# Attention and two feed-forward blocks on one core: one transpose for both heads' first 64 keys

## The chip, the cores and the metric

The kernel runs on one core of a Trainium2 chip. The metric is device time in microseconds (us). The kernel before takes 504.18 us, the median of 3 runs (503.7 to 505.47).

## The reference

Causal attention over 2 sequences of 448 tokens with 12 heads of 64, then two feed-forward blocks on the 896 tokens of width 768. All inputs and outputs are fp32.

```python
# attention: q, k, v are (2, 12, 448, 64)
scores = np.matmul(q, k.transpose(0, 1, 3, 2)) / np.sqrt(64)
scores = np.where(np.triu(np.ones((448, 448), bool), k=1), -1e9, scores)
scores = scores - scores.max(-1, keepdims=True)
attn = np.exp(scores)
attn = attn / (attn.sum(-1, keepdims=True) + 1e-09)
x = np.matmul(attn, v).transpose(0, 2, 1, 3).reshape(896, 768)
# first block: w_in (768, 2048), w_out (2048, 768), alpha (2048,)
h = x @ w_in
y = (np.maximum(h, 0) + alpha * np.minimum(h, 0)) @ w_out
# second block: w1, w2, w3, w_out2 (768, 768)
out = np.maximum(np.maximum(y @ w1, y @ w2), y @ w3) @ w_out2
```

## The kernel before, in words

Nothing is issued in the order in which it is written. Each step (a load, a group of matmuls, one elementwise instruction) is given to a planner (`Plan`, L71) with a rank, the engines that could run it and a cost on each, the steps it follows, and the ring buffers it takes and gives back. `Plan.run` (L146) then issues, again and again, the step that can start first on its clock, and among equals the one with the lowest rank. The order on each engine is fixed when the kernel is built; at run time an engine takes its own list in order and waits on semaphores.

Attention is 12 jobs (`Job`, L463), one for a sequence and a pair of heads j = 0, 1. The 448 queries are cut into four chunks c of 64, 128, 128 and 128 rows (`START`, L228), and the keys in the same way. Because the mask is causal, chunk c has scores with its first `START[c+1]` keys alone: 64, 192, 320 or 448. A job goes through these steps:

- Two loads: `qk` (448 KB, L558) and `v` (256 KB, L562), from SyncE's queue.
- Scores (`scores`, L564) in two steps of two chunks, first 448 and 64 columns, then 320 and 192. The two heads use the two halves of TensorE's rows, 64 each, side by side. A step takes two of four PSUM banks (ring `s`).
- For each chunk and head: the masked row maximum on VectorE (L595), the exponential with its row sum on ScalarE (L608), per step one reciprocal on VectorE (L619, L620), and the scaling on GpSimd (L624). All of this is in place in the tile `e`, which holds first all of head 0, then all of head 1.
- Transposes (`p_t`, L633) by TensorE, in three groups per head: the first 64 keys (4 transposes that give 64 rows), key chunks 1 and 3 (4), and key chunk 2 (2). That is 20 per job. Each group is copied from PSUM (ring `t`, 3 banks) to the tile `p` by VectorE (L287) or ScalarE (L281): 6 copies per job. The upper half of the rows of the first group in `p` is zeroed once (L449).
- The product with V (`av`, L648, called AV below): 8 matmuls, for the 4 key chunks and the 2 heads, of 448, 384, 256 and 128 columns. The two heads use the two halves of TensorE's columns, side by side. The result is split in two parts for the next block (`xh` L281, `xl` L293).

Every fp32 matmul of scores and AV stands in the trace as two records (two passes); a transpose is one.

The feed-forward blocks multiply split numbers: each product is three matmuls (L406), high by high, high by low and low by high. A weight matrix is split by ScalarE and VectorE (and sometimes GpSimd) into such a pair, in a ring of four (`w`). Products of w_in whose weights are ready early are put between the steps of the last jobs (fill). After attention TensorE does the rest of the first block, the second block and the stores; the 896 tokens go as a piece of 512 and one of 384 columns, always in this order.

At the start TensorE does 8 products on a tile of zeros (`warm`, L711), which VectorE has to write first (L259). A small load brings `alpha` on ScalarE's queue (L274).

Of the kernel before, what the change touches and what calls it, by code (L numbers as in the profile page):

```python
# [23 lines left out]
RINGS = dict(w=4, m=1, s=4, t=3, v=4, qk=3, e=3, p=4)  # L24
NB = 5
HELD = 4
WARM = 8
# [3 lines left out]
    load=-6, s=12, max=12, exp=16, recip=10,  # L31
# [39 lines left out]
class Plan:  # L71
# [27 lines left out]
    def add(  # L99
        self, rank, engines, fn, after=(), take=(), give=(), delay=0.0, port=False, mode="full"  # L100
    ):
# [6 lines left out]
        self.waiting[i] = (rank, engines, fn, after, tuple(take), give, delay, port, mode)  # L108
        self.open[i] = sum(d in self.waiting for d in after)
        for d in after:  # L110
            self.next.setdefault(d, []).append(i)
        if not self.open[i]:
            self.ready[i] = None
        return i

    def start(self, step):
# [12 lines left out]
        for engine, took in engines.items():  # L129
# [6 lines left out]
            if engine == "PE" and mode != self.mode:  # L136
# [9 lines left out]
    def run(self):  # L146
        while self.waiting:
# [20 lines left out]
            if engine == "PE":  # L168
                self.mode = mode
# [18 lines left out]
def attention_moe_moe2_kernel(  # L188
# [73 lines left out]
    mask = first.tile([P, S], F32, name="mask")  # L262
    nc.gpsimd.memset(mask, 0.0)
    nc.gpsimd.affine_select(
        out=mask[:, S - P :],
        in_=mask[:, S - P :],
        compare_op=ALU.is_ge,
        fill=FILL,
        base=0,
        pattern=[[-1, P]],  # L270
        channel_multiplier=1,
    )
    alpha_sb = const.tile([P, KF], F32, name="alpha_sb")
    nc.scalar.dma_start(out=alpha_sb, in_=alpha)  # L274
# [133 lines left out]
    class Product:  # L408


        def __init__(self, rank, pieces, bank, token):

            total = len(pieces)
            self.end = None
            for i, (count, n, terms, after, give) in enumerate(pieces):
                self.end = plan.add(
                    rank,
# [19 lines left out]
    BANKS = ((0,), (1, 3), (2,))  # L437
    AT_COL, BANK_COL = {}, [0]
# [7 lines left out]

    p_all = [at.tile([P, BANK_COL[-1]], F32, bufs=1, name=f"p{i}") for i in range(RINGS["p"])]
    for p in p_all:
        nc.vector.memset(p[ROWS[0] :, : BANK_COL[1]], 0.0)  # L449
# [4 lines left out]
    e_all = [at.tile([P, 2, NP], F32, bufs=1, name=f"e{i}") for i in range(RINGS["e"])]  # L454
    for e in e_all:
        nc.vector.memset(e[ROWS[0] :, :, : OFF[1]], 0.0)
    used = {"p": 0, "e": 0}
# [5 lines left out]
    class Job:  # L463


        def __init__(self, rank, b, hp):
            self.b, self.hp = b, hp
            self.ps, self.pt, self.p = {}, {}, {}

            def add(kind, *args, **kw):  # L470
# [3 lines left out]
            load_v = add("load", on_dma(256), step(self.load_v), take=("v",), delay=1.8)  # L474

            norm = [[], []]
            s = None
            for i, cs in enumerate(PAIRS):
# [7 lines left out]
                    give=(("qk", load_qk),) * (i == len(PAIRS) - 1),  # L486
# [21 lines left out]
                for c in cs:  # L508
                    for j in range(2):
                        took = on_pool(START[c + 1], two=False)  # L510
                        if b * HP + hp < FIRST:
                            took |= on_dve(START[c + 1], fast=True)
                        norm[j].append(
                            add("norm", took, partial(self.normalize, i, c, j), (r,), port=True)
# [3 lines left out]
            for j in range(2):  # L518
                for n in range(len(BANKS)):
                    w = BANK_COL[n + 1] - BANK_COL[n]  # L520
                    keys = sum(ROWS[kc] for kc in BANKS[n] for c in range(kc, NCH))
                    t = add(
                        "p",
                        {"PE": keys * 0.85e-3 + 0.03},
                        step(self.p_t, j, n),
                        norm[j] if t is None else [*norm[j], t],
                        take=("t",) + ("p",) * (n == 0),
                        give=(("e", e_took),) * (j == 1 and n == len(BANKS) - 1),
                    )
                    if n == 0:  # L530
                        p_took.append(t)
                    src = partial(self.pt.get, (j, n))
                    outs.append(
                        add(
                            "p_out",
                            on_dve(w, psum=True) | on_act(w, psum=True),
                            copy(partial(self.p_part, j, n), src),
                            (t,),
                            give=(("t", t),),
                        )  # L540
                    )
            a = add(
                "av",
                {"PE": 4 * BANK_COL[-1] / 2400},
# [3 lines left out]
                mode="columns",  # L548
                give=(*(("p", x) for x in p_took), ("v", load_v)),
# [14 lines left out]
        def scores(self, i):  # L564
# [6 lines left out]
            for c in PAIRS[i]:  # L571
                n = START[c + 1]
                for j in range(2):
# [7 lines left out]
                        self.qk[d, 1, :n],  # L581
# [5 lines left out]
        def e_part(self, c, j):  # L587
            return self.e[: ROWS[c], j, OFF[c] : OFF[c + 1]]

        def column(self, tile, i, c, j):  # L590
            return tile[: ROWS[c], 2 * i + PAIRS[i].index(c), j : j + 1]

        def row_max(self, i, c, j):
            n, m = START[c + 1], S - P + ROWS[c]
# [3 lines left out]
                in1=mask[: ROWS[c], m - n : m],  # L598
# [18 lines left out]
        def recip(self, i):  # L617
            sm = self.sm[:, 2 * i : 2 * i + 2, :]
# [14 lines left out]
        def p_t(self, j, n):  # L633
            if n == 0:
                self.p[j] = turn("p", p_all)
            keys = ROWS[BANKS[n][0]]
            pt = ps_t.tile([P, BANK], F32, tag="t", name="pt")
            self.pt[j, n] = pt[:keys, : BANK_COL[n + 1] - BANK_COL[n]]
# [374 lines left out]
```

## Time and profile before

| | |
|---|---|
| median of 3 runs | 504.18 us |
| the profiled execution | 504.13 us, span 502.3 us (1.8 us lie around the span) |
| attention, first scores to last AV | 4.25 to 101.03 us |
| feed-forward matmuls after it | 101.03 to 498.97 us |
| TensorE busy | 495.1 us, 99% of the span |
| ScalarE, VectorE, GpSimd busy | 256.9, 360.6, 63.5 us |

The busy time of TensorE is modelled, so the chain of waits is read beside it: it tells which engine the end of the program depended on at each time. PE is TensorE's matmul, PEld its loading of the stationary operand, DVE is VectorE, ACT is ScalarE, POOL is GpSimd, SP is SyncE. In the tables x16 means 16 records merged.

### The profile page before, as it was taken

How to read it: one execution, taken by the hardware profiler on the slowest of the kernel's cores; microseconds unless marked ns; L12 is line 12 of the kernel's file. 1: busy time of each engine (PE TensorE's matmuls, PEld its weight loads, DVE VectorE, ACT ScalarE, POOL GpSimd, SP SyncE). 2: the span in 40 equal slices, each digit the busy share in tenths (PEclk: the TensorE clock that was granted, in tenths of full speed). 3: DMA queues.
4: the chain of work that ended last, by engine and by line, in shares of the span. 5: the costliest groups of instructions: out<-in, count | busy, mean ns of one | idle time of the engine just before them, and what ended most of it. 6: DMA issues, size and time to landing. Idle time of an engine off the chain costs nothing.

```text
span 502.3 us, 7218 instructions
## 1 busy us (share of the span) xinstructions
PE 495.1 (99%) x2684; PEld 427.5 (85%) x2684; DVE 360.6 (72%) x727; ACT 256.9 (51%) x502; POOL 63.5 (13%) x113
## 2 busy tenths in 40 slices
PE   8999999999999999999999999999999999999997
PEld 5665666789989899898899899898899899889997
DVE  7889878859999999968557467579999896601000
ACT  5999898645453555434425335366566544401111
POOL 3657755330100000000000000000000000000000
PEclk9999999999999999999999999999999999999999
DMA  7635410213332333333333343253554443000111
GB/s 255 234 88 173 154 44 13 111 67 125 127 126 78 112 127 105 116 115 106 115 116 104 93 138 122 69 185 128 188 186 160 157 134 118 1 1 31 64 64 63
DMA packets 14147, 56.70 MB, mean 113 GB/s; under 512 B 1696, under 2 KB 3488, under 8 KB 14112
## 3 DMA queue, kind: packets, MB, share of 16 engines
q1 hardware_dynamic: 13968, 56.24, 33.7%
q8 instruction: 21, 0.34, 0.3%
q14 instruction: 14, 0.11, 0.1%
q10 hardware_dynamic: 144, 0.01, 0.0%
HBM read 53.49 MB, written 2.75 MB: 112 GB/s over the span
## 4 chain that ended last, share of the span: by engine, by line
PE 94%; DVE 3%; ACT 2%; issue 0%; DVEq 0%
PE ps L406 81%; PE pt L643 4%; PE pv L652 4%; PE ps L578 4%; DVE e L595 2%; ACT e L608 1%; DVE sm L619 1%; PE warm L714 1%; DVE p L287 0%; ACT p L281 0%; DVE sm L620 0%; ACT o L281 0%; DVE nm L595 0%; ACT xh L281 0%; DVE zeros L259 0%
## 5 line engine op out<-in xcount | busy, mean ns | idle before, releaser
L406 PE MATMUL ps<-xh,wh 128*128 128x384 f32 (+2 forms) x408 | 149.4, 366 | 0.0
L406 PE MATMUL ps<-xh,wl 128*128 128x384 f32 (+2 forms) x408 | 148.7, 364 | 0.0
L406 PE MATMUL ps<-xl,wh 128*128 128x384 f32 (+2 forms) x408 | 148.5, 364 | 0.0
L406 PEld LDWEIGHTS ps<-xh,wh 128*128 128x128 f32 x408 | 76.7, 188 | 8.4 <-DVE xl L293 0.3
L406 PEld LDWEIGHTS ps<-xl,wh 128*128 128x128 f32 x408 | 76.6, 188 | 8.1
L406 PEld LDWEIGHTS ps<-xh,wl 128*128 128x128 f32 x408 | 76.5, 188 | 7.8
L281 ACT CAST wh<-t 128x768 fp32r<-128x768 f32 (+1 forms) x53 | 43.0, 811 | 73.3 <-DVE t L401 73.0
L406 PE MATMUL ps<-g_h,wl 128*128 128x512 f32 (+1 forms) x192 | 70.0, 365 | 0.0
L406 PE MATMUL ps<-g_l,wh 128*128 128x512 f32 (+1 forms) x192 | 69.9, 364 | 0.0
L406 PE MATMUL ps<-g_h,wh 128*128 128x512 f32 (+1 forms) x192 | 69.6, 362 | 0.0
L369 ACT ACTIVATE t<-raw 128x768 f32<-128x768 f32 (+1 forms) x59 | 52.3, 887 | 14.0 <-DMA raw<-in_moe_w_dram 5.0
L293 DVE TENSOR_TENSOR wl<-t,wh 128x768 fp32r<-128x768 f32 (+1 forms) x47 | 43.3, 921 | 21.9 <-ACT wh L281 21.9
L390 DVE SCALAR_TENSOR_TENSOR t<-raw,t 128x768 uint32<-128x768 uint32 (+1 forms) x59 | 54.7, 927 | 0.9
L401 DVE CUSTOM_DVE_ANT_0 t<-t,r 128x1536 uint16<-128x1536 uint16 (+1 forms) x57 | 52.6, 924 | 2.2
L387 ACT ACTIVATE r<-raw 128x768 uint32<-128x768 uint32 (+1 forms) x59 | 52.0, 881 | 4.1 <-DMA raw<-in_moe_w_dram 3.1
L608 ACT ACTIVATE e<-e,nm 128x448 f32<-128x448 f32 (+3 forms) x96 | 47.8, 503 | 5.1 <-DVE nm L595 4.9
L624 POOL TENSOR_SCALAR e<-e,sm 128x448 f32<-128x448 f32 (+3 forms) x96 | 45.6, 494 | 31.2 <-DVE sm L620 12.5
L406 PEld LDWEIGHTS ps<-g_l,wh 128*128 128x128 f32 x192 | 36.0, 188 | 4.1
L406 PEld LDWEIGHTS ps<-g_h,wh 128*128 128x128 f32 x192 | 36.1, 188 | 4.1
L406 PEld LDWEIGHTS ps<-g_h,wl 128*128 128x128 f32 x192 | 36.0, 188 | 3.8
L281 ACT CAST g_h<-g 128x512 fp32r<-128x512 f32 (+2 forms) x32 | 18.1, 567 | 39.2 <-DVE g L686 39.0
L595 DVE CUSTOM_DVE_ANT_0 e<-ps,mask 128x448 f32<-128x448 f32 (+3 forms) x96 | 35.2, 413 | 4.1 <-PE ps L578 3.9
(53 smaller groups left out, 584.0 us busy)
## 6 DMA issues: line engine op xcount, KB each, us to landing
raw<-in_moe_w_dram SPq DMA_DIRECT2D x18, 768.0 KB, 4.3
raw<-in_moe_w_in_dram SPq DMA_DIRECT2D x17, 768.0 KB, 4.4
raw<-in_moe_w_out_dram SPq DMA_DIRECT2D x12, 768.0 KB, 4.4
raw<-in_moe_w_out_dram SPq DMA_DIRECT2D x12, 640.0 KB, 4.1
qk<-in_qk_dram SPq DMA_DIRECT2D x12, 448.0 KB, 3.5
v<-in_v_dram SPq DMA_DIRECT2D x12, 256.0 KB, 2.7
out_dram<-o SPq DMA_DIRECT2D x14, 192.0 KB, 1.9
alpha_sb<-in_moe_alpha_dram ACTq DMA_DIRECT2D x1, 8.0 KB, 3.5
```

What stands on the lines that cost most here:

```text
L281: nc.scalar.copy(out(), src())
L293: ENGINE[engine].tensor_tensor(out=out(), in0=a(), in1=f32(b()), op=ALU.subtract)
L369: nc.scalar.activation(out=f32(self.t), in_=f32(self.raw[..., 1]), func=AF.Abs)
L387: nc.scalar.activation(out=self.r, in_=self.raw[..., 0], func=AF.Copy, scale=2.0**-29)
L390: nc.vector.scalar_tensor_tensor(out=self.t, in0=self.raw[..., 1], scalar=0xC0000000, in1=self.t, op0=ALU.bitwise_and, op1=ALU.bitwise_or,)
L401: ENGINE[engine].tensor_tensor(out=t, in0=t, in1=self.r.bitcast(I32), op=ALU.add)
L406: nc.tensor.matmul(ps, a, c, start=(first and y == 0), stop=(last and y == 2))
L578: nc.tensor.matmul(ps, self.qk[d, 0, START[c] : START[c] + P], self.qk[d, 1, :n], start=True, stop=True,)
L595: nc.vector.tensor_tensor_reduce(out=self.e_part(c, j), in0=self.ps[c, j], in1=mask[: ROWS[c], m - n : m], op0=ALU.add, op1=ALU.min, scale ...
L608: nc.scalar.activation(out=s, in_=s, func=AF.Exp, scale=-1.0, bias=self.column(self.nm, i, c, j), accum_out=self.column(self.sm, i, c, j),)
L624: ENGINE[engine].tensor_scalar(out=s, in0=s, scalar1=self.column(self.sm, i, c, j), scalar2=1.0, op0=ALU.mult, op1=ALU.mult,)
L643: nc.tensor.transpose(pt[:keys, o : o + P], self.e[:, j, s : s + keys], ident)
```

## The change

What it does, part by part:

1. The keys (and V) of head 0 are laid out backwards by the host, so that head 0's first 64 keys stand last in its piece of a chunk's row. In `e`, the two heads' pieces of one chunk now stand next to each other, so the first 64 keys of both heads are 128 neighbouring columns. Head 0 gets a mirrored mask of its own. One group of 4 transposes of 128 columns takes the place of the two heads' 4 + 4 of 64: 16 transposes and 5 copies per job. The group comes last and its result goes to a tile `p0` of its own.
2. AV begins with one matmul over all of TensorE (128 rows of `p0` and of V, 448 columns, both heads at once, L680); the other six stay as they were (L685). The planner is told that this step enters TensorE's whole array and leaves it in columns.
3. The first job's scores go in three steps, 192 and 64 columns first, then 320, then 448, with three reciprocals.
4. The opening products read a constant in place of the zeroed tile, and are 9 in place of 8. The memsets of `zeros` and `p` go.
5. V's loads have their own rank, behind the next job's `qk`; `alpha` comes on SyncE's queue.
6. After attention, the pieces of 512 and 384 tokens alternate in order from one weight tile to the next.

```diff
-RINGS = dict(w=4, m=1, s=4, t=3, v=4, qk=3, e=3, p=4)
+RINGS = dict(w=4, m=1, s=4, t=3, v=4, qk=3, e=3, p0=2, p=4)
-WARM = 8
+WARM = 9
-    load=-6, s=12, max=12, exp=16, recip=10,
+    load=-6, v=12, s=12, max=12, exp=16, recip=10,
...
-    zeros = first.tile([P, S], mybir.dt.bfloat16, name="zeros")
-    nc.vector.memset(zeros, 0.0)
+    ones = nc.const_aps.tensor(1.0, [P, S], mybir.dt.bfloat16)
...
-    BANKS = ((0,), (1, 3), (2,))
+    BANKS = ((2,), (1, 3))
...
-    for p in p_all:
-        nc.vector.memset(p[ROWS[0] :, : BANK_COL[1]], 0.0)
...
+            self.groups = ((1, 0), (2,), (3,)) if rank == 0 else PAIRS
...
-            load_v = add("load", on_dma(256), step(self.load_v), take=("v",), delay=1.8)
+            load_v = add("v", on_dma(256), step(self.load_v), take=("v",), delay=1.8)
...
+            parts = [(j, kcs) for j in range(2) for kcs in BANKS] + [(0, (0,))]
+            for j, kcs in parts:
+                heads = (0, 1) if 0 in kcs else (j,)
...
-                {"PE": 4 * BANK_COL[-1] / 2400},
+                {"PE": 4 * (S + BANK_COL[-1]) / 2400 + plan.SWITCH},
...
-                    nc.tensor.transpose(pt[:keys, o : o + P], self.e[:, j, s : s + keys], ident)
+                    s = 2 * OFF[c] + START[c + 1] + (START[kc] if j else -START[kc + 1])
+                    nc.tensor.transpose(pt[:, o : o + P], self.e[:, s : s + P], ident)
...
-            for kc in range(NCH):
+            nc.tensor.matmul(
+                pv, self.v[:, 0].rearrange("p j d -> p (j d)"), self.p0, start=True, stop=False
+            )
+            for kc in range(1, NCH):
...
+    def to_and_fro(i, cut):
+        return [(u, cut[u]) for u in (range(len(cut)) if i % 2 == 0 else reversed(range(len(cut))))]
...
-        us = SEQ[1:] if f < NB else CUT
+        us = SEQ[1:] if f < NB else [t for _, t in to_and_fro(f, CUT)]
```

On TensorE, from the third job's scores to the first AV and a little beyond, the kernel before has these instructions. L578 is the scores, L643 the transposes (of the tile `e` of job 0, `e_126`), L652 the AV.

```order
L578 MATMUL ps<-qk 128x448 x2
L578 MATMUL ps<-qk 128x64 x2
L578 MATMUL ps<-qk 128x320 x2
L578 MATMUL ps<-qk 128x192 x2
L643 MATMUL pt<-ident,e_126 64x128 x4
L643 MATMUL pt<-ident,e_126 128x128 x6
L643 MATMUL pt<-ident,e_126 64x128 x4
L643 MATMUL pt<-ident,e_126 128x128 x6
L578 MATMUL ps<-qk 128x448 x2
L578 MATMUL ps<-qk 128x64 x2
L652 MATMUL pv<-p_112,v 64x448
L652 MATMUL pv<-p_113,v 64x448
```

The same place in the changed kernel; L601 is the scores, L670 the transposes (`e_120` of job 0, `e_121` of job 1), L680 and L685 the AV.

```order
L601 MATMUL ps<-qk 128x64 x2
L670 MATMUL pt<-ident,e_120 128x128 x6
L601 MATMUL ps<-qk 128x320 x2
L601 MATMUL ps<-qk 128x192 x2
L670 MATMUL pt<-ident,e_120 128x128 x10
L601 MATMUL ps<-qk 128x448 x2
L601 MATMUL ps<-qk 128x64 x2
L670 MATMUL pt<-ident,e_121 128x128 x2
L680 MATMUL pv<-p_279,v 128x448
L685 MATMUL pv<-p,v 64x384 x2
L685 MATMUL pv<-p,v 64x256 x2
L685 MATMUL pv<-p,v 64x128 x2
```

Job 0's first six transposes now stand ahead of job 2's second scores; four transposes of 20 are gone; two of job 1 stand ahead of the first AV, and the AV has one matmul of the whole array in front.

GpSimd's scaling of the first job (`e_126`) before:

```order
L624 TENSOR_SCALAR e_126<-e_126,sm_120 128x448 x2
L624 TENSOR_SCALAR e_126<-e_126,sm_120 64x64 x2
L624 TENSOR_SCALAR e_126<-e_126,sm_120 128x320 x2
L624 TENSOR_SCALAR e_126<-e_126,sm_120 128x192 x2
L624 TENSOR_SCALAR e_127<-e_127,sm_121 128x448 x2
```

And in the changed kernel (`e_120`):

```order
L649 TENSOR_SCALAR e_120<-e_120,sm_114 128x192 x2
L649 TENSOR_SCALAR e_120<-e_120,sm_114 64x64 x2
L649 TENSOR_SCALAR e_120<-e_120,sm_114 128x320 x2
L649 TENSOR_SCALAR e_120<-e_120,sm_114 128x448 x2
L649 TENSOR_SCALAR e_121<-e_121,sm_115 128x448 x2
```

The shortest rows come first and the 448-wide last, in step with the scores.

## Rows read from the trace of the kernel before

**Rows 1.** Page, part 1: busy us, share, instructions.

```profile
PE 495.1 (99%) x2684; PEld 427.5 (85%) x2684; DVE 360.6 (72%) x727; ACT 256.9 (51%) x502; POOL 63.5 (13%) x113
```

**Rows 2.** Chain of waits, after attention: start us, us, what.

```profile
101.03 397.94 PE ps L406 x2004
```

**Rows 3.** Two stretches: us, PE, PEld, DVE, ACT, POOL busy, clock, DMA, GB/s.

```profile
30.00:45.00 15.00, 15.00 (x115) 9.80 (x113) 13.50 (x54) 14.43 (x45) 7.98 (x16) 1.00 0.46 143
...
125.00:200.00 75.00, 75.00 (x375) 67.61 (x374) 73.35 (x116) 37.63 (x54) 1.85 (x1) 1.00 0.34 112
```

**Rows 4.** Chain of waits, in attention (pt transposes, ps scores, pv AV).

```profile
16.12 3.94 ACT e L608 x16
...
27.17 0.58 PE pt L643 x4
...
28.82 2.36 PE pt L643 x20
31.18 1.12 PE ps L578 x8
32.30 2.20 PE pv L652 x16
...
49.42 0.60 DVE p L287
...
51.12 0.44 PE pt L643 x4
...
75.71 1.97 PE pt L643 x18
...
92.73 2.20 PE pv L652 x16
```

**Rows 5.** Timeline of PEld in the first AV: start us, us, what.

```profile
17.73 0.14 PEld L652 LDWEIGHTS pv<-p,v 128*64 128x64 f32 x2 [0.23 <-issue]
18.11 0.14 PEld L652 LDWEIGHTS pv<-p,v 128*64 128x64 f32 x2 [0.23 <-issue]
```

**Rows 6.** Groups by form: the transposes' loads, an exponential, copies | busy, mean ns.

```profile
L643 PEld LDWEIGHTS pt<-ident,e 128*128 128x128 f32 x144 | 16.1, 140 | 5.8 <-issue 2.5 <-DVE p L287 2.1 <-ACT p L281 0.4
...
L608 ACT ACTIVATE e<-e,nm 128x448 f32<-128x448 f32 x24 | 15.8, 662 | 4.5 <-DVE nm L595 4.4
...
L643 PEld LDWEIGHTS pt<-ident,e 128*64 128x64 f32 x96 | 10.0, 111 | 2.0 <-issue 0.9 <-POOL e L624 0.3 <-ACT p L281 0.2
...
L281 ACT COPY p<-pt 64x448 f32<-64x448 f32 x15 | 7.7, 526 | 3.5 <-PE pt L643 3.3
...
L287 DVE COPY p<-pt 64x448 f32<-64x448 f32 x9 | 5.5, 607 | 1.3 <-PE pt L643 1.3
```

**Rows 7.** Timeline of the opening, 0 to 18 us.

```profile
1.15 3.17 PE L714 MATMUL warm<-zeros 128*128 128x448 bf16 x8 [1.15 <-DVE zeros L259]
...
4.25 0.51 PEld L578 LDWEIGHTS ps<-qk 64*128 64x128 f32 x4 [0.73 <-DMA qk<-in_qk_dram]
...
6.19 0.62 DVE L595 CUSTOM_DVE_ANT_0 e<-ps,mask 128x448 f32<-128x448 f32 x1 [2.43 <-PE ps L578]
...
6.74 0.62 DVE L595 CUSTOM_DVE_ANT_0 e<-ps,mask 128x448 f32<-128x448 f32 x1
...
7.28 0.21 DVE L595 CUSTOM_DVE_ANT_0 e<-ps,mask 64x64 f32<-64x64 f32 x1
...
7.57 0.48 DVE L595 CUSTOM_DVE_ANT_0 e<-ps,mask 128x320 f32<-128x320 f32 x1
...
10.04 3.63 POOL L624 TENSOR_SCALAR e<-e,sm 128x448 f32<-128x448 f32 x8 [7.96 <-ACT e L608]
...
13.58 2.67 PE L643 MATMUL pt<-ident,e 128*64 128x128 f32 x20
...
17.30 2.27 PE L652 MATMUL pv<-p,v 128*64 128x448 f32 x16
```

**Rows 8.** Waits: engine waiting <- waited for: us in total, times, longest.

```profile
PE pt L643 <- DVE p L287: 1.2, 2, 0.7
```

More of the change, by code (lines that the diff above doesn't have):

```diff
@@ L99, in add @@
     def add(
-        self, rank, engines, fn, after=(), take=(), give=(), delay=0.0, port=False, mode="full"
+        self,
+        rank,
+        engines,
+        fn,
+        after=(),
+        take=(),
+        give=(),
+        delay=0.0,
+        port=False,
+        mode="full",
+        leaves=None,
     ):
@@ L107, in add @@
         after = tuple(dict.fromkeys(after))
-        self.waiting[i] = (rank, engines, fn, after, tuple(take), give, delay, port, mode)
+        self.waiting[i] = (rank, engines, fn, after, tuple(take), give, delay, port, (mode, leaves or mode))
         self.open[i] = sum(d in self.waiting for d in after)
@@ L255, in attention_moe_moe2_kernel @@
     plan.buffers(**RINGS, raw=2, ct=2, cr=2, eg=2)
[L258 to L259 removed]
+    ones = nc.const_aps.tensor(1.0, [P, S], mybir.dt.bfloat16)
     ident = first.tile([P, P], F32, name="ident")
     make_identity(nc, ident)
[L262 to L271, printed above, removed]
[L272 to L274 removed]
+    masks = []
+    for j, o in enumerate((0, S - P)):
+        mask = first.tile([P, S], F32, name=f"mask{j}")
+        nc.gpsimd.memset(mask, 0.0)
+        nc.gpsimd.affine_select(
+            out=mask[:, o : o + P],
+            in_=mask[:, o : o + P],
+            compare_op=ALU.is_ge,
+            fill=FILL,
+            base=0 if j else 1 - P,
+            pattern=[[-1 if j else 1, P]],
+            channel_multiplier=1,
+        )
+        masks.append(mask)
+    alpha_sb = const.tile([P, KF], F32, name="alpha_sb")
+    alpha_load = plan.add(
+        50,
+        on_dma(8),
+        step(nc.sync.dma_start, alpha_sb, alpha),
+        delay=1.8,
+    )
     ENGINE = {"ACT": nc.scalar, "DVE": nc.vector, "POOL": nc.gpsimd}
@@ L512, in __init__ @@
                             took |= on_dve(START[c + 1], fast=True)
-                        norm[j].append(
-                            add("norm", took, partial(self.normalize, i, c, j), (r,), port=True)
+                        norm[c, j] = add(
+                            "norm", took, partial(self.normalize, i, c, j), (r,), port=True
                         )
             t, outs, p_took = None, [], []
[L518 to L528, printed above, removed]
-                    )
[L530 to L541, printed above, removed]
@@ new lines, in __init__ @@
+            parts = [(j, kcs) for j in range(2) for kcs in BANKS] + [(0, (0,))]
+            for j, kcs in parts:
+                w = sum(S - START[kc] for kc in kcs)
+                heads = (0, 1) if 0 in kcs else (j,)
+                ring = "p0" if 0 in kcs else "p"
+                first = 0 in kcs or kcs == BANKS[0]
+                done = [norm[c, h] for c in range(min(kcs), NCH) for h in heads]
+                t = add(
+                    "p",
+                    {"PE": sum(NCH - kc for kc in kcs) * 0.11 + 0.03},
+                    step(self.p_t, j, kcs),
+                    done if t is None else [*done, t],
+                    take=("t",) + (ring,) * first,
+                    give=(("e", e_took),) * (0 in kcs),
+                )
+                if first:
+                    p_took.append((ring, t))
+                outs.append(
+                    add(
+                        "p_out",
+                        on_dve(w, psum=True) | on_act(w, psum=True),
+                        copy(partial(self.p_part, j, kcs), partial(self.pt.get, (j, kcs))),
+                        (t,),
+                        give=(("t", t),),
+                    )
+                )
@@ L547, in __init__ @@
                 take=("t",),
-                mode="columns",
-                give=(*(("p", x) for x in p_took), ("v", load_v)),
+                give=(*p_took, ("v", load_v)),
+                leaves="columns",
             )
@@ L570, in scores @@
             at_col = 0
[L571 removed]
+            for c in self.groups[i]:
                 n = START[c + 1]
@@ L693, in part @@
             return g[f][i][:, u]
-        n = plan.add(rank, {"DVE": 0.13 + N / 960}, step(neg), (prod.end,), take=("eg",))
+        n = plan.add(rank, {"DVE": 0.13 + N / 960}, step(neg), (prod.end, alpha_load), take=("eg",))
         p = plan.add(rank, on_dve(N), step(pos), (n,), give=((token, prod.took),))
@@ L713, in warm @@
         for _ in range(WARM):
-            nc.tensor.matmul(ps, zeros[:, :P], zeros, start=True, stop=True)
+            nc.tensor.matmul(ps, ones[:, :P], ones, start=True, stop=True)
     plan.add(0, {"PE": WARM * 0.36}, step(warm), take=("m",), give=(("m", None),))
```

95 lines of the change are left out of this document (55 added, 40 removed).

## The prediction

> **What bounds the kernel now.** I read the page's busy shares first: TensorE is busy in 99% of the span [rows 1]. That share is modelled, so I went on to the chain of waits. From 101.03 us on it is one piece of 397.94 us, 2004 feed-forward matmuls without a gap [rows 2]. Nothing on any other engine matters there unless it makes TensorE wait, and all columns of this stretch stay as they are. In attention the chain also stays on TensorE most of the time: a job is transposes, scores, AV, again and again; it leaves it for ScalarE's exponentials from 14 to 22 us and for VectorE from 43 to 50 [rows 4]. The table of stretches then shows who is close behind: from 30 to 45 us ScalarE is busy for 14.43 of 15.00 us and VectorE for 13.50; from 125 to 200 us VectorE for 73.35 of 75 [rows 3]. So a microsecond of TensorE work taken out of attention should end the program a microsecond sooner, as long as ScalarE and VectorE keep up. The opening is different: TensorE does not reach its first transpose until 13.58 us [rows 7].
>
> **Transposes.** The chain shows 18 transposes, some of either width, behind a feed-forward product, in 1.97 us: 0.109 us each; four of 64 behind such a product take 0.44, which is the same [rows 4]. So width does not matter and only the count does. 20 become 16 in each of 12 jobs: 48 x 0.109 = 5.2 us less.
>
> The Trainium skill, page "TensorE: Matmul & The Clock Gate", section "LDWEIGHTS (loading the stationary operand)", speaks against this: a load takes as long as its columns are many, columns / 1.2 ns, by which an estimate is 53 ns for 64 and 107 ns for 128. If loads set the pace, four wide ones would cost what eight narrow ones did, and this term would be 0. The trace disagrees in size: the two loads last 111 and 140 ns [rows 6], not one to two, and the pace is 0.109 for both. I keep this as rival D.
>
> **AV.** The first matmul of the two heads, side by side, becomes one of the whole array with as many columns. No fp32 product of the whole array stands in the trace. The nearest row is the AV's own second pass of 448 columns, which gives way to the next after 18.11 - 17.73 = 0.38 us [rows 5]; the pair of heads takes two such passes, and I take two for the joint one: cost 0. The ends: a single pass would save 0.38 x 12 = 4.6 us, four passes would add 0.76 x 12 = 9.1. I see no reason for either, since both operands stay fp32.
>
> What does cost is one more change of the array's shape. Four transposes behind an AV take 0.58 us, four behind a full-array product 0.44 = 4 x 0.109 [rows 4]: leaving columns costs 0.14. Twenty behind scores take 2.36, less 2.18: 0.18. An AV takes 2.20 us behind scores and behind transposes alike [rows 4]; its passes of 448, 384, 256 and 128 columns at the pace of [rows 5] make 2.06, so entering columns costs about 0.14 too. In the order of instructions I count the changes of shape from the first transpose on (transpose to feed-forward product and back are free): 51 before, 62 after, since all 12 AVs change shape inside, 7 of them come straight from scores, and the split of transposes adds a few. 11 x 0.17 = 1.9 us more (ends 1.5 and 2.9, at 0.14 and at the 0.26 by which 1.12 us for first scores [rows 4] exceeds their passes).
>
> **Opening.** Scores start when `qk` lands: the wait at 4.25 us is for that DMA [rows 7]. The opening products no longer wait for VectorE's zeros (start 1.15 us) but are one more at about 0.37 us, so they end where they did; if they start no earlier, scores come 0.3 us later. The first step now has 256 columns in place of 512 for each head; by the distance from 4.25 to VectorE's start at 6.19 us, and with a first pass at the slow pace there, I put VectorE's start at 5.65. From the starts of [rows 7] a row maximum takes 0.55 us for 448 columns, 0.15 for 64, 0.41 for 320, and by those 0.28 for 192. Two of 192, two of 64 and two of 320 end at 7.3; the 448-wide scores need the first step's banks, free at 6.5, and are there at 7.7. One maximum (8.2) and one reciprocal (some 0.3) later GpSimd starts at 8.65, not 10.04. Its eight products take 3.63 us as before, so head 0 is done at 11.7 and head 1 at 12.3.
>
> TensorE does job 2's first scores ahead of the transposes, and these need banks that VectorE clears at 11.1; they end at 12.0. First transposes at 12.1 instead of 13.58. From there, with job 2's second scores, ten transposes, job 3's first scores and two transposes of job 1, the first AV stands at 16.4, not 17.30: 0.9 us sooner. The four transposes fewer (0.44, counted above) and the two pulled ahead and two changes of shape (0.22 + 0.35, against it) about cancel, so idle time of TensorE falls by 0.9 us. The ends: 0, if some step of this walk waits for its engine; 1.5, if the whole lead of the first transposes is kept.
>
> **At nothing.** The copies: 24 of 64 rows (0.53 us on ScalarE, 0.61 on VectorE [rows 6]) become 12 of 128 rows and the same length. They lie beside TensorE and shorten its followers. The memsets that go and the second mask that comes lie in the time before 6.19 us in which VectorE waited 2.43 us for the first scores. V's loads stand behind the next job's `qk` on SyncE's queue, the first behind one more, at the very start, and its AV comes at 16 us. `alpha` is needed by the first fill product, tens of us later; on SyncE it stands behind the fourth V, ahead of the first weights. The 9 fill matmuls that the order no longer has before the last AV (48 before, 39 after) are done behind it at the same price. The alternating order changes neither columns nor loads; between pieces of 512 and 384 the chain had no gap [rows 2]. VectorE's weight splitting from 125 to 200 us is close to full, but a new weight waits for a buffer that TensorE frees, so it moves forward with TensorE; if that cover failed, up to the 4 us gained would be lost there.
>
> **More waits.** After its opening TensorE waited 1.2 us in two places for a copy by VectorE [rows 8]. It will ask faster now, while ScalarE is nearly full [rows 3] and VectorE's copies stand in the chain near 49 us [rows 4]; between 0 and once more the same 1.2 I add 0.5 us.
>
> **Sum,** against the profiled execution of 504.13 us (its span is 502.3, with 1.8 around it, and the median of the runs is 504.18): - 5.2 + 1.9 - 0.9 + 0.5 = - 3.7. Forecast 500.4 us.
>
> **Rivals.**
> A. ScalarE and VectorE set the pace in attention. For: 14.43 of 15.00 us [rows 3], and the chain's stretches on either [rows 4]. Against: TensorE waited there for 1.2 us in all [rows 8], and both start sooner by the 0.5 us of the opening and have 12 copies less to do. Then attention shrinks only by their own saving, 12 copies of 0.53 to 0.61 us over two engines, 3.4 us, plus the 0.9 of the opening, less the 9 fill matmuls (0.2 each, 1.8) that no longer fit in: 2.4 us, 501.7. Chance 0.16.
> B. A new wait: AV waits for the copy of the joint group, which now comes last, is 448 wide and not 256, and holds both heads. Between that group and its AV stand job scores of 1.12 us [rows 4]; the copy takes 0.53 and may stand behind an exponential of 0.66 us [rows 6]. Behind one, AV is late by 0.12 us; behind two, by 0.78. At a mean of 0.34 us in 11 jobs the whole gain is gone. At 0.3 it is 503.7, no change (chance 0.10); at 0.78, 8.6 us, it is 509.0, slower (chance 0.04). For it: the place is new and tight; against: before, a last copy stood there too, and in the chain an AV follows TensorE's own scores or transposes [rows 4].
> C. The waits of [rows 8] go, and the opening keeps all 1.5: 500.4 - 0.5 - 1.2 - 0.6 = 498.1. Chance 0.10.
> D. Loads set the pace of transposes: the term of 5.2 is 0, 505.6. Chance 0.02.
>
> **How the numbers follow.** Forecast 0.56, by itself 499.2 to 501.3; A 0.18; B 0.14; C 0.10; D 0.02. About 0.3%, 1.5 us, is what a measurement here can tell from no change, so faster means under 502.7: forecast, A and C, 0.84. Same is B's smaller end, 0.10; slower B's larger end and D, 0.06. The range leaves out B, D and the far end of C: 498.4 to 502.7. Four passes of the joint product would lie outside it, as would a single one.
>
> **What would show it.** Transposes 192 records and still 0.109 us apart; the joint product two records of 0.38 us; the first maximum near 5.65, GpSimd near 8.65, first transposes near 12.1, the first AV near 16.4; the last AV some 6 us sooner than before, with 9 more matmuls in the last piece of the chain, which still has no gap. I am wrong if the last piece breaks up, if an AV waits for a copy, if the joint product takes more than 0.8 us, or if TensorE's waits in attention exceed some 3 us.

## The result, and the profile after

The changed kernel takes 499.20 us, the median of 5 runs (499.06 to 499.46); its ratio to the kernel before is 0.990, with a 95% interval of 0.9886 to 0.9914. The profiled execution took 499.39 us with a span of 497.6. Against 504.13 and 502.3 us that is 4.74 us less.

First the page's busy shares and the chain of waits of the changed kernel (start, length, engine and line; L601 scores, L670 transposes, L680 and L685 AV, L425 feed-forward).

```profile
PE 490.8 (99%) x2613; PEld 422.2 (85%) x2613; DVE 359.3 (72%) x725; ACT 249.8 (50%) x489; POOL 65.9 (13%) x115
```

```profile
15.14 1.12 PE ps L601 x8
16.26 0.37 PE pt L670 x2
16.63 0.75 PE pv L680 x2
17.38 1.45 PE pv L685 x12
...
20.48 1.54 PE pt L670 x12
22.02 1.12 PE ps L601 x8
23.14 0.95 PE pv L680 x2
24.09 1.45 PE pv L685 x12
...
94.13 1.45 PE pv L685 x12
95.58 398.64 PE ps L425 x2013
```

Three things are to be seen beside [rows 2, 4]. The last AV ends at 95.58 us and not 101.03, 5.45 sooner. The last piece is whole, as before, and holds 2013 matmuls, 9 more than the 2004 of [rows 2]; 9 products of 448 columns at 0.203 us are 1.83, so attention itself is 5.45 - 1.83 = 3.6 us shorter. And the last piece is 398.64 us where 397.94 + 1.83 = 399.77 was due: 1.1 us less for the same columns. 3.6 + 1.1 is the whole gain. An AV behind transposes takes 0.75 + 1.45 = 2.20 us as before, one behind scores 0.95 + 1.45 = 2.40. Ten transposes in one piece take 1.09, the 0.109 us each of before:

```profile
70.58 1.09 PE pt L670 x10
```

The opening in the timeline (start, duration, engine, operation; in brackets the idle time before and what ended it), beside [rows 7]:

```profile
0.77 3.52 PE L751 MATMUL warm<-const-bfloat16-1.0 128*128 128x448 bf16 x9 [0.77 <-PEq L1038]
5.24 0.36 DVE L619 CUSTOM_DVE_ANT_0 e<-ps,mask 128x192 f32<-128x192 f32 x1 [3.80 <-PE ps L601]
8.30 3.66 POOL L649 TENSOR_SCALAR e<-e,sm 128x192 f32<-128x192 f32 x8 [5.45 <-DVE sm L645]
11.96 0.88 PE L670 MATMUL pt<-ident,e 128*128 128x128 f32 x6
16.46 0.92 PE L680 MATMUL pv<-p,v 128*128 128x448 f32 x2
```

Two rows of TensorE's waits from 12 to 96 us (total, times, longest) answer to [rows 8], and the two stretches of [rows 3] show ScalarE and VectorE as busy as before, and GpSimd busier (11.53 us of 15, from 7.98).

```profile
PE ps L425 <- DVE g L723: 0.6, 1, 0.6
PE pt L670 <- DVE p L306: 0.5, 1, 0.5
```

```profile
30.00:45.00 15.00, 14.87 (x98) 8.57 (x99) 14.08 (x59) 14.56 (x48) 11.53 (x21) 1.00 0.45 151
125.00:200.00 75.00, 75.00 (x377) 68.02 (x376) 73.87 (x118) 35.91 (x52) 1.74 (x1) 1.00 0.31 103
```

### The profile page after: what moved, and what is told of

The parts are those of the page before. It is cut to its first block, busy times and chain, and to the rows that moved or that the text cites. A ratio compares the mean times of both kernels' runs of the same rounds, so it can differ in the third digit from the quotient of the medians.

```text
span 497.6 us, 7099 instructions
## 1 busy us (share of the span) xinstructions
PE 490.8 (99%) x2613; PEld 422.2 (85%) x2613; DVE 359.3 (72%) x725; ACT 249.8 (50%) x489; POOL 65.9 (13%) x115
## 4 chain that ended last, share of the span: by engine, by line
PE 96%; DVE 3%; issue 0%; ACT 0%; DVEq 0%
PE ps L425 81%; PE ps L601 5%; PE pt L670 4%; PE pv L685 3%; PE pv L680 2%; PE warm L751 1%; DVE e L619 1%; DVE sm L644 0%; DVE p L306 0%; DVE xl L312 0%; DVE t L420 0%; DVE t L409 0%; DVE g L723 0%; DVE g L713 0%; ACT xh L300 0%
## 5 line engine op out<-in xcount | busy, mean ns | idle before, releaser
L425 PE MATMUL ps<-xh,wh 128*128 128x384 f32 (+2 forms) x408 | 149.0, 365 | 0.6 <-DVE g L723 0.6
L425 PE MATMUL ps<-xh,wl 128*128 128x384 f32 (+2 forms) x408 | 148.3, 364 | 0.0
L425 PE MATMUL ps<-xl,wh 128*128 128x384 f32 (+2 forms) x408 | 148.1, 363 | 0.0
L425 PEld LDWEIGHTS ps<-xh,wh 128*128 128x128 f32 x408 | 76.6, 188 | 9.0 <-DVE g L723 0.8
L425 PEld LDWEIGHTS ps<-xl,wh 128*128 128x128 f32 x408 | 76.6, 188 | 7.9
L425 PEld LDWEIGHTS ps<-xh,wl 128*128 128x128 f32 x408 | 76.6, 188 | 7.9
L425 PE MATMUL ps<-g_h,wl 128*128 128x512 f32 (+1 forms) x192 | 69.9, 364 | 0.0
L425 PE MATMUL ps<-g_l,wh 128*128 128x512 f32 (+1 forms) x192 | 69.8, 363 | 0.0
L425 PE MATMUL ps<-g_h,wh 128*128 128x512 f32 (+1 forms) x192 | 69.6, 362 | 0.0
L420 DVE CUSTOM_DVE_ANT_0 t<-t,r 128x1536 uint16<-128x1536 uint16 (+1 forms) x56 | 51.5, 923 | 2.1
L632 ACT ACTIVATE e<-e,nm 128x192 f32<-128x192 f32 (+3 forms) x96 | 47.7, 500 | 6.7 <-DVE nm L619 6.7
L649 POOL TENSOR_SCALAR e<-e,sm 128x192 f32<-128x192 f32 (+3 forms) x96 | 47.4, 513 | 24.2 <-DVE sm L645 18.9
L425 PEld LDWEIGHTS ps<-g_l,wh 128*128 128x128 f32 x192 | 36.0, 188 | 4.1
L425 PEld LDWEIGHTS ps<-g_h,wh 128*128 128x128 f32 x192 | 36.1, 188 | 4.0
L425 PEld LDWEIGHTS ps<-g_h,wl 128*128 128x128 f32 x192 | 36.0, 188 | 3.8
L619 DVE CUSTOM_DVE_ANT_0 e<-ps,mask 128x192 f32<-128x192 f32 (+3 forms) x96 | 35.3, 412 | 5.1 <-PE ps L601 5.0
L300 ACT CAST g_h<-g 128x384 fp32r<-128x384 f32 (+2 forms) x32 | 18.1, 567 | 37.3 <-DVE g L723 34.6
```

The lines of the kernel that those rows point to most:

```text
L300: nc.scalar.copy(out(), src())
L420: ENGINE[engine].tensor_tensor(out=t, in0=t, in1=self.r.bitcast(I32), op=ALU.add)
L425: nc.tensor.matmul(ps, a, c, start=(first and y == 0), stop=(last and y == 2))
L619: nc.vector.tensor_tensor_reduce(out=self.e_part(c, j), in0=self.ps[c, j], in1=masks[j][: ROWS[c], m : m + n], op0=ALU.add, op1=ALU.min, s ...
L632: nc.scalar.activation(out=s, in_=s, func=AF.Exp, scale=-1.0, bias=self.column(self.nm, i, c, j), accum_out=self.column(self.sm, i, c, j),)
L649: ENGINE[engine].tensor_scalar(out=s, in0=s, scalar1=self.column(self.sm, i, c, j), scalar2=1.0, op0=ALU.mult, op1=ALU.mult,)
```

## The experiments

Each was timed beside the kernel before on one chip, in three sets (before took 503.95 us in that of e1 to e4, 504.46 in that of e5 to e8, 504.18 in that of e9 to e12). Where a microsecond matters, kernels of different sets are compared by their ratios.

| kernel | median us | ratio to before, 95% interval |
|---|---|---|
| the change | 499.20 | 0.990 [0.9886, 0.9914] |
| e1_order_back | 500.82 | 0.9935 [0.9923, 0.9948] |
| e2_joint_only | 512.00 | 1.0159 [1.0145, 1.0173] |
| e3_two_steps | 513.64 | 1.0191 [1.0177, 1.0204] |
| e4_columns | 497.55 | 0.9869 [0.9855, 0.9882] |
| e5_fill_in_one | 498.91 | 0.9895 [0.9879, 0.991] |
| e6_transposes_twice | 503.21 | 0.9976 [0.9967, 0.9985] |
| e7_joint_fill_in_one | 500.50 | 0.9923 [0.9911, 0.9936] |
| e8_columns_fill_in_one | 498.42 | 0.9888 [0.9875, 0.9902] |
| e9_before_alternating | 503.47 | 0.9982 [0.9973, 0.9991] |
| e10_before_fill_in_one | 503.18 | 0.9977 [0.9967, 0.9987] |
| e11_change_fill_in_one | 499.97 | 0.9909 [0.9896, 0.9923] |
| e12_both_spared | 502.56 | 0.996 [0.9947, 0.9972] |

### The alternating order: e1_order_back, e9_before_alternating

The first undoes part 6 in the changed kernel, the second does part 6 alone in the kernel before.

```diff
-        us = SEQ[1:] if f < NB else [t for _, t in to_and_fro(f, CUT)]
+        us = SEQ[1:] if f < NB else CUT
...
-            for u, cut in to_and_fro(KG + f + i + 1, CUT):
+            for u, cut in enumerate(CUT):
```

> The changed kernel with part 6 undone: the pieces of 512 and 384 tokens come in the same order always, attention is instruction for instruction that of the changed kernel. Theory P: the feed-forward stage's 1.1 us that I had not forecast come from the alternating order; this run takes 500.3 us and its last piece of the chain is about 399.8 us for 2013 matmuls. Rival Q: they come from elsewhere (where tiles lie, or the chance of one execution); this run takes 499.2 us, as the changed kernel.

> The kernel before with the sixth part of the change alone: the pieces of 512 and 384 tokens alternate in order. In the traces so far, the ten or so matmuls behind a change of width are slower than the others by 38 ns in all (384 to 512) and by 29 ns (512 to 384), alike in four kernels; with 42 pairs of changes against 28 among the last 1700 matmuls. Theory P (the gain behind attention, 1.1 us, is these changes of width): 0.9 to 1.1 us less than before, attention as before, 503.0 to 503.4 us where before takes 504.2. Rival: the gain needs the joint transposes (other work beside the matmuls): no change.

The last row but two of each chain, of the first kernel and of the second:

```profile
96.05 399.65 PE ps L425 x2013
```

```profile
101.44 396.88 PE ps L406 x2004
```

399.65 against 398.64 for the same 2013 matmuls, 396.88 against 397.94 for the same 2004: 1.0 and 1.1 us, so the order of the pieces is the whole of the gain behind attention, with or without the joint transposes. In time, e9 is 0.7 us faster, a little less than the 0.9 to 1.1 expected; its attention ended 0.4 us later in the profiled execution, with the same instructions, and e1's 0.5 us later than the change's. That half microsecond comes from the opening (below).

### Parts taken alone, and what became of them: e2_joint_only, e3_two_steps

The first keeps parts 1 and 2 alone; the second takes only part 3 out of the change.

```diff
-            self.groups = ((1, 0), (2,), (3,)) if rank == 0 else PAIRS
+            self.groups = PAIRS
```

> Parts 1 and 2 alone (joint transposes, joint first product of AV); parts 3 to 6 undone. Theory: TensorE's work sets the end. By the order, transposes and changes of shape come to 3.75 us less than in the kernel before, the opening keeps its first transposes near 13.6 us and gains nothing: 500.5 to 501. Rival: the opening or the feed-forward order carries the gain, and joint transposes little: 502.5 or more.

> The changed kernel with part 3 undone: the first job's scores in two steps, 448 columns first. Theory: the first transposes and the first AV come 0.9 us later, and the other order saves 0.4 us of shape changes: 499.7 us. Rival: the opening is not on the path, since the later waits for VectorE set the pace: 498.8 to 499.2 us.

Both are misses by 11 to 14 us: slower than the kernel before. In attention nothing was lost; in e3 it ended at 94.45 us, 1.1 sooner than in the change, with 6 fill matmuls (1.2 us) fewer in it. The loss stands behind it. The chain of e3 from there on, with the pieces of TensorE and what lies between the last two:

```profile
125.09 26.32 PE ps L425 x120
...
151.43 0.84 ACT wh L300
...
152.30 0.96 DVE wl L312
...
159.64 1.01 DVE g L723 x2
...
160.69 347.77 PE ps L425 x1746
```

ScalarE's row of waits from 95 to 200 us, in e3 (the changed kernel has no such row there):

```profile
ACT wh L300 <- PE ps L425: 18.4, 4, 7.2
```

TensorE waits for ScalarE and VectorE, and these for TensorE. `wh` is ScalarE's cast of a new weight into a buffer of the ring of four; it waits for a matmul that still reads the old one, and VectorE's split, the prelu of the last product and the freeing of its PSUM bank stand behind it in their fixed order. The timeline shows who still reads: between a product of 384 columns and one of 512 stands a single step of three matmuls with 448.

```profile
116.80 0.33 PE L425 MATMUL ps<-xh,wl 128*128 128x384 f32 x1
116.97 0.36 PE L425 MATMUL ps<-xh,wh 128*128 128x448 f32 x1
117.18 0.37 PE L425 MATMUL ps<-xl,wh 128*128 128x448 f32 x1
117.38 0.37 PE L425 MATMUL ps<-xh,wl 128*128 128x448 f32 x1
117.59 0.40 PE L425 MATMUL ps<-xh,wh 128*128 128x512 f32 x1
```

That is a leftover of the fill, which uses one PSUM bank, so one held matrix after the other. In e3 its last step starts at 184.5 us, in the change at 149.0, in the kernel before at 152.7. The series starts later since the first weight split is ready at 58.4 us, not 46.9: with joint transposes and two steps of scores in the first job the planner put the casts elsewhere (the kernel before, also with two steps, has it at 49.3). At 122 us, just ahead of the wait that ends at 125.09, twelve such steps are still to come in e3, those of two held matrices; in the change there are seven. So two of four weight buffers are still in use there, and the last is read some 35 us longer.

Why the planner walked into this can be read from the code, though no run changed it: a held matrix gives its buffer back with the product of the second sequence's columns (L812 of the changed kernel, L775 of the kernel before), the 72 matmuls of 448 right behind attention, and not with its last leftover step. On the planner's clock the buffer is free; at run time the cast waits for the step that still reads it.

Two explanations were left: the held buffers (F), or VectorE, idle early (31.36 of 37 us busy from 13 to 50 us, against 35.18) and then behind (W).

### The leftover steps put together: e5_fill_in_one, e7_joint_fill_in_one, and a control, e10_before_fill_in_one

```diff
                     take=(token,) if i == 0 else (),
                     give=give,
+                    delay=-plan.SAME * (token == "m"),
```

Here `m` is the fill's one PSUM bank and `plan.SAME` the 0.12 us that the planner puts between a step and the next that follows it on the same engine. e5 is e3 with this line, e7 is e2 with it, e10 the kernel before with it.

> The kernel with the first job's scores in two steps took 513.64 us, and the reason is open. In it a matrix of w_in that is held over attention is still read at 165 us: its six steps of 3 matmuls stand one by one between the products of 18, since the planner puts a step that follows another on TensorE 0.12 us behind it and finds a whole product that could start sooner. Here that delay is taken off these steps alone, so that they follow one another without anything between; by the planner's clock the last one then starts at 111 us and not at 168, while the first split of weights stays as late as it was (near 58 us, against 47 after the change). Theory F: the held matrices keep two of the four weight buffers, ScalarE's cast into the next buffer waits for TensorE (18.4 us of such waits there, 0 after the change), VectorE's work stands behind it and TensorE then waits for that. It expects these waits under 3 us, no gap of TensorE behind attention, and 498.8 to 500.5 us. Rival W: VectorE falls behind because it works less in attention's first half (31.4 us of 37, against 35.2) and the first split is late; that stays, so 511 to 514 us.

> The joint transposes and the joint product alone (the kernel of 512.0 us), with the held matrices' steps following one another as in the other run. Theory F: 500.0 to 501.3 us, which is the forecast's terms of transposes, shape changes and waits without the opening (504.2 - 5.2 + 1.9 + 0.5 = 501.4), less up to 1 us that the steps put together may save in changes of order. Rival W: 510 to 512.5 us.

> The kernel before with the held matrices' steps following one another and nothing else, as a control: it has 0.3 us of ScalarE's waits for a weight buffer, so theory F sees nothing to gain: 503.5 to 504.7 us. If it came under 503, the steps put together would be worth something by themselves, and the two kernels that they mended would have to be read against that.

513.64 became 498.91 us and 512.0 became 500.5, both inside what F expected. ScalarE's row and the end of the chain in e5:

```profile
ACT wh L300 <- PE ps L425: 2.6, 1, 2.6
```

```profile
94.51 399.21 PE ps L425 x2016
```

Early on nothing changed. The busy time of the engines (PE, PEld, DVE, ACT, POOL, then granted clock, DMA share and GB/s) from 13 to 50 us and from 112 to 160, first e3, then e5:

```profile
13.00:50.00 37.00, 36.88 (x261) 23.57 (x257) 31.36 (x140) 35.91 (x122) 23.22 (x52) 1.00 0.49 151
112.00:160.00 48.00, 41.43 (x196) 36.12 (x194) 37.66 (x58) 18.43 (x26) 1.85 (x1) 0.96 0.28 95
```

```profile
13.00:50.00 37.00, 36.88 (x261) 23.52 (x259) 31.34 (x140) 35.88 (x122) 23.12 (x52) 1.00 0.49 150
112.00:160.00 48.00, 48.00 (x240) 43.50 (x239) 45.81 (x72) 21.45 (x31) 0.00 (x0) 1.00 0.32 107
```

VectorE's early idle time is the same, its first split as late (58.1 us), and the loss is gone: W falls, F stands. The control was not quite the zero that I expected. It is 1.0 us faster (0.9977): attention holds 6 more fill matmuls (1.2 us) and ends only 0.5 us later, the waits of [rows 8] falling from 1.2 to 0.5. So some 0.7 to 1.0 us of what e5 and e7 gained may be the line by itself; the other 10 to 14 are the buffers.

### What a transpose costs: e6_transposes_twice

```diff
-                    nc.tensor.transpose(pt[:, o : o + P], self.e[:, s : s + P], ident)
+                    for _ in range(1 + (0 in kcs)):
+                        nc.tensor.transpose(pt[:, o : o + P], self.e[:, s : s + P], ident)
```

> After the change, each of the four joint transposes of a job is issued twice in a row to the same place, 48 more in all, with everything else and its order on every engine as it was. Theory T (TensorE sets attention's length, and a transpose costs it 0.109 us): 48 x 0.109 = 5.2 us, 504.4 us; with the 0.4 us of waits that remain between transposes and AV as the only cover, 504.0 to 504.6. Rival V (the vector engines set attention's pace and TensorE's transposes lie beside them): under 501.5 us.

The end of attention moved from 95.58 to 99.37 us, by 3.8, and the time by 3.8 to 4.0 (by the ratios and by the medians); expected was 5.2, and not under 4.8. The table of two stretches, of the change and then of e6, shows the rest:

```profile
13.00:50.00 37.00, 36.39 (x253) 22.89 (x252) 35.18 (x142) 35.59 (x117) 26.42 (x51) 1.00 0.55 180
50.00:95.60 45.60, 44.92 (x296) 29.49 (x294) 40.19 (x124) 36.66 (x106) 29.57 (x45) 1.00 0.30 98
```

```profile
13.00:50.00 37.00, 37.00 (x262) 24.05 (x262) 34.24 (x138) 34.51 (x114) 25.63 (x49) 1.00 0.54 168
50.00:99.40 49.40, 49.23 (x335) 33.84 (x333) 41.67 (x130) 38.40 (x110) 30.38 (x47) 1.00 0.31 100
```

TensorE's idle time falls from 0.61 + 0.68 to 0.00 + 0.17 us: 1.1 us of the extra transposes went into waits that were there. V (under 501.5) falls, and T holds for about three quarters of the added work; the waits that I had taken for cover were too few, since I counted only the 0.4 us between transposes and AV.

### The change of shape inside AV: e4_columns, e8_columns_fill_in_one

AV's first product goes back to two halves of TensorE's columns, on the same joint tile and the same rows of V.

```diff
-            nc.tensor.matmul(
-                pv, self.v[:, 0].rearrange("p j d -> p (j d)"), self.p0, start=True, stop=False
-            )
+            for j in range(2):
+                nc.tensor.matmul(
+                    pv[D * j : D * j + D], self.v[:, 0, j, :], self.p0, start=True, stop=False
+                )
```

> The changed kernel with AV's first product done in two halves of TensorE's columns, side by side, on the same joint tile (V is zero in the other head's rows), so that AV has no change of shape inside. Theory: a joint product costs two passes of 0.38 us, just as the pair does, and the change of shape inside AV 0.14 to 0.2 us more; by the order of instructions 1.2 us less on TensorE: 498.0 us. Rival: what TensorE saves is lost in waits for VectorE's copies near 40 to 49 us: 499.2 us.

> The kernel with AV's first product in two column halves (497.55 us), with the held matrices' steps following one another. It had 2.7 us of ScalarE's waits for a weight buffer, none of which reached TensorE. Theory F: nothing is left to gain, 497.0 to 498.0 us. Rival: if waits behind attention cost it a part of its time even there, under 496.8 us; if the new order puts other work late, over 498.5 us.

497.55 us, the best of all kernels here, 1.6 less than the change. An AV behind scores in its chain:

```profile
49.05 1.12 PE ps L601 x8
50.17 0.90 PE pv L681 x4
51.07 1.29 PE pv L686 x12
```

2.19 us, against 2.40 in the change; behind transposes both take 2.20. Seven AVs of the change follow scores directly: 7 x 0.2 = 1.4 of the 1.6 us. That is an estimate, since the planner's order differs too: five AVs of e4 follow scores, and TensorE waits 0.4 us for others in its attention where the change has 1.1. With the fill steps put together as well it was no better: 498.42, outside the 497.0 to 498.0 expected. In its trace one AV waits 0.8 us for VectorE's copy of transposes, and two rows of its stretches show TensorE waiting 1.3 us at attention's end for the last split of x.

```profile
92.60:94.00 1.40, 0.09 (x2) 0.02 (x1) 1.28 (x3) 0.58 (x1) 0.74 (x1) 1.00 0.90 364
94.00:97.00 3.00, 3.00 (x15) 2.80 (x16) 1.09 (x2) 0.57 (x1) 1.08 (x1) 1.00 0.06 25
```

### Three steps or two: e11_change_fill_in_one, e12_both_spared

e11 is the change with the line of e5, e12 has that line, two steps of scores and the column halves.

> The whole change with the held matrices' steps following one another. Theory F: no waits for buffers to take away, 498.6 to 499.8 us. Beside the same with two steps of scores in the first job (498.91 us, where before took 504.46), it tells what three steps are worth by themselves: 0.9 us less (498.0) if the forecast's walk through the opening holds, about the same (498.9) if the opening's lead is lost behind the first AV, whose start differed by 0.4 us between two executions of the same instructions.

> The change with two steps of scores in the first job, AV's first product in two column halves, and the held matrices' steps following one another. If the terms add (498.91 us for the second and the third, 1.6 us less for the halves): 497.3 us, as good as the best so far (497.55). If all fill steps are done before attention ends, TensorE waits at its end for the last split of x by VectorE, 1.3 us as in the kernel with columns and fill in one: 498.4 us.

e11 took 499.97 us, e5 498.91 in another set; by ratios, 0.9909 and 0.9895, whose intervals overlap. So three steps as planned here bring nothing that shows. One AV of e11 waits 0.7 us for ScalarE's copy of transposes, none of e5 does, so part of what they might bring is lost in the new order. The starts of the first row maximum and the first AV tell why:

| | first maximum, us | first AV, us | between |
|---|---|---|---|
| before, e9, e10 | 6.19, 6.58, 6.27 | 17.30, 17.71, 17.41 | 11.11 to 11.14 |
| joint, two steps: e2, e3, e5, e7 | 6.24, 6.32, 5.97, 5.62 | 16.91, 16.98, 16.64, 16.28 | 10.66 to 10.67 |
| the change, e1, e11 | 5.24, 5.70, 5.70 | 16.46, 16.92, 16.93 | 11.22 to 11.23 |

The distance is the same to 0.03 us within a row of the table. Joint transposes shorten it by 0.45, four transposes; three steps bring the first maximum sooner and give 0.56 of it back on the way to AV. These 0.56 are what the prediction had against them: two transposes of job 1 pulled ahead (0.22) and two changes of shape more (0.35). When the first maximum starts differs by more than 0.6 us between executions of one opening (6.24 and 5.62 in e2 and e7): that is the scatter of a single profile.

e12 missed: 502.56, not 497.3 or 498.4. TensorE waited 2.4 us for one prelu by VectorE, and worked at half its clock behind it (last section). Its first weight split is ready later still, at 64.4 us; why the prelu was late was not tried.

## Why the prediction was right, and where a size was off

499.2 us lies in the range (498.4 to 502.7), 1.2 under the forecast and at the lower end of what it gave the forecast by itself (499.2 to 501.3). Point by point, between the two profiled executions:

| term | forecast | measured |
|---|---|---|
| 48 transposes fewer | -5.2 | -5.2 by the pace, which is still 0.109 us (1.09 for 10, in one piece of the chain) |
| more changes of shape | +1.9 | +1.4 for AVs behind scores (7 x 0.20); the other four at 0.17, not measured apart, make it +2.1 |
| opening | -0.9 | first AV 0.84 sooner in this execution, 0.38 in e1 and 0.37 in e11, which have the same opening |
| more waits | +0.5 | -0.1: TensorE idle 1.35 us from 13 to 101 us before, 1.29 from 13 to 95.6 after |
| attention | -3.7 | -3.6 |
| behind attention | 0 | -1.1 |

The four measured terms add to -4.0 and attention is only 3.6 us shorter: 0.4 us were spent that none of these terms holds, and where was not shown.

**The term that was mis-sized** is the one put at nothing: "The alternating order changes neither columns nor loads". That is so, and the last piece still has no gap; but its matmuls are not all equally long, and e1 and e9 put 1.0 and 1.1 us on the order.

**In part luck.** The first AV came out at 16.46 for 16.4 forecast, but not by the walk that led there: the first maximum stood at 5.24 for 5.65 and the way from it to the AV took 11.22 for 10.75. In e1 and e11, with the same opening, the first maximum is at 5.70, GpSimd starts at 8.75 (8.65 forecast), the first transposes stand at 12.41 (12.1 forecast; 11.96 in the change) and the first AV at 16.92. So the walk was right up to GpSimd and 0.5 us short behind it, and this execution began 0.46 us sooner. Nor does a gain of three steps show in the times (e11 and e5). The added waits did not come by the profile; 0.4 us that no term holds stand in their place, so the sum for attention is right to 0.1 in part by chance. The joint product is two records, as taken, and costs nothing behind transposes. The copy of 128 rows of 448 takes 0.54 us on ScalarE and 0.61 on VectorE, the length of the 64 rows of before, as taken.

**Parts 1 and 2** by themselves, with the buffers' loss out of the way on both sides, are e7 against e10: 500.50 against 503.18, ratios 0.9923 and 0.9977, some 2.7 us (each ratio's interval is 0.5 to 0.6 us to either side). The forecast's terms for them make - 5.2 + 1.9 + 0.5 = - 2.8. With 1.0 for the order these are 3.7 of the change's 5.0 us. Parts 4 and 5 had no run of their own: e5, which leaves out part 3 alone, is 1.4 us ahead of e7, and with 1.0 of these for the order 0.4 is left to them, inside the intervals. What the rest of the 5.0 is was not shown; with the fill steps put together on both sides, the whole change (e11 against e10) is worth 3.4.

**The cover that I named was real.** "If that cover failed, up to the 4 us gained would be lost there", I wrote of the weight splitting. In the changed kernel it holds. In e2 and e3 it fails, and the price was 11.5 us (e2 less e7) and 14.7 (e3 less e5), not 4: I had left out that ScalarE, VectorE and TensorE wait in a ring, and what a long wait does to TensorE's clock. That the change holds is luck too: it rests on how the planner happened to place the first casts with three steps in the first job, and part 3, of no worth that shows in the opening, decides 14 us that way.

**The rivals.** A: TensorE's waits did not grow, so the vector engines do not set the pace as a whole; e6 found 1.1 us in which they do. (In the chain of before, others than TensorE also stand from 58.6 to 62.3 us, a stretch that the prediction does not name.) B: the one wait of an AV for a copy in the changed kernel's trace is 0.2 us; that it can come is shown by e8 and e11, with 0.8 and 0.7. C: the waits of [rows 8] fell from 1.2 to 1.1 alone, and the first AV came 0.84 sooner and not 1.5. D: 128 columns now throughout, and the same 0.109 us. The Trainium skill, page "TensorE: Matmul & The Clock Gate", section "LDWEIGHTS (loading the stationary operand)", gives columns / 1.2 ns for a load, 107 for these and 53 for the 64 of before. The pace of 0.109 us agrees with it for 128 columns and not for 64, which were as slow [rows 4]; the load records themselves last 140 and 111 ns [rows 6]. The prediction gives A a chance of 0.16 in one place and 0.18 in another; with 0.18 its chances add to 1.

## What to carry to other kernels

Where a planner fixes every engine's order, an edit is also a new order: time a part alone before crediting it, and when a part makes things worse by more than it could cost, look for a ring of waits in which one engine's cast waits for a buffer that another still reads. A few leftover steps that hold a buffer are better done together than one at a time. A gapless chain says that TensorE never waits, not that each matmul takes its least.

## What the hardware showed that I had not expected

**A change of width slows the matmuls behind it.** Distances between the starts of neighbouring records among the last 1700 matmuls, averaged by place behind a change, in ns above the settled distance (227 for 512 columns, 173 for 384), in the kernel before; in the change and in e1 and e4 each number is the same to 0.3:

```
place behind the change     1     2     3     4     5     6     7     8     9    10
384 to 512               +2.3  +6.3  +8.8  -2.8  +3.8  +8.8  +1.3  +5.5  +3.8  -0.4
512 to 384               -2.2  +2.0  +4.5 +12.0  +2.8  +8.7  +0.3  +0.3  +0.4  +0.3
```

Some 38 and 29 ns for each change. The kernel before has 42 of each in this stretch, the changed one 28: 14 x 67 = 0.9 us of the 1.1. What makes them slow was not tried.

**TensorE's clock after a wait.** Two rows of e12, four of e3 and two of e2, stretches cut at the waits (after the busy times, the granted clock as a share of 2.4 GHz):

```profile
86.90:89.90 3.00, 0.62 (x7) 0.38 (x5) 2.93 (x6) 1.82 (x4) 1.10 (x2) 1.00 0.53 209
89.90:93.00 3.10, 3.10 (x9) 1.42 (x11) 3.07 (x3) 0.94 (x2) 0.82 (x1) 0.52 0.16 33
```

```profile
122.60:125.10 2.50, 0.71 (x3) 0.28 (x3) 2.08 (x4) 1.19 (x2) 0.00 (x0) 1.00 0.00 0
125.10:128.10 3.00, 3.00 (x7) 2.34 (x8) 2.97 (x6) 1.33 (x2) 0.00 (x0) 0.53 0.20 37
...
155.00:160.70 5.70, 0.33 (x3) 0.01 (x1) 5.68 (x10) 2.00 (x4) 0.00 (x0) 0.89 0.44 138
160.70:163.00 2.30, 2.30 (x6) 1.98 (x7) 2.30 (x5) 2.18 (x3) 0.00 (x0) 0.50 0.01 4
```

```profile
128.00:130.20 2.20, 0.43 (x2) 0.01 (x1) 2.20 (x6) 0.88 (x3) 1.71 (x1) 1.00 0.55 229
130.20:133.20 3.00, 2.99 (x17) 2.94 (x18) 2.97 (x6) 2.18 (x3) 0.10 (x1) 1.00 0.00 0
```

Behind waits of TensorE of 2.4 us (e12), 1.8 and 5.4 (e3) the granted clock is 0.50 to 0.53, the lower of its two levels, 1.2 GHz, for 3 to 5 us, and matmuls of 512 columns stand 0.43 us apart in place of 0.227. Behind the wait of 1.3 us in e8 it stays at 1.00, and so it does in e2 behind a wait of the same 1.8 us: the length of the wait alone does not tell. Where the clock fell, it cost about half of the wait or more once again: 3 us at half pace lose 1.5 behind the 1.8 and the 2.4, and 5.3 lose 2.6 behind the 5.4. In e3 TensorE's three waits behind attention (1.4, 1.8 and 5.4) make 8.6 us and the clock some 4 of the 14.7 that e5 got back.
